# Attention and a multiplicative feed-forward on one core: q of batch 1 turned by transfers, the x product on other PSUM tiles, another listing, the last block of out cut at column 320

## The chip, the core and the metric

The kernel runs on one core of one Trainium2 chip. The metric is the device time of one execution in microseconds (us).

## The reference

```python
q_s = softmax over d of q          # (8 batches, 8 heads, 576 tokens, 64)
k_s = softmax over the tokens of k
kv  = einsum('bhsd,bhse->bhde', k_s, v)
x   = einsum('bhsd,bhde->bhse', q_s, kv)  ->  (4608 tokens, 512)
out = ((x @ w1) * (x @ w2)) @ w3 @ w_out  # w1, w2: 512x1024, w3: 1024x1024, w_out: 1024x512
```

Both softmaxes subtract a maximum and add 1e-9 to the sum. Inputs and the output are float32.

## The kernel before

Every step of the kernel has a name, and the order in which all steps are emitted is written out by hand in the listing `ORDER` (lines 77 to 146). Each engine runs its own steps in the order of that listing; where a step can run on one of several engines, the table `PICKS` (lines 154 to 210) names the engine. `Plan.run` walks the listing and emits each step. Nothing is reordered later, so a step that waits holds up everything behind it on its engine.

The steps, by name (the numbers behind a name are batch or chunk, then part):

- **Loads.** `w1`, `w2` (four column pieces each), `w3` (six row pieces), `wo` (two halves of w_out), `k.b`, `q.b`, `v.b`. The first batches and all weights are issued by POOL in the order of the table `LOADS` (line 217); a load waits until the one eight places before it has landed (line 433). The two parts of q of batch 0 and, later, the batches of the table `LATE` (line 224) are issued by SP. The first of LATE, `q.2`, waits for the load `w1.3`. A batch in the table `APART` (line 265) is loaded in two halves.
- **The fold.** For each of the eight row blocks `ft` of w3: `w3t` transposes it on PE, `w3T` copies that to SBUF, `pf.ft.0` and `pf.ft.1` (four matmuls of 512 columns each) multiply it with the two halves of w_out, and `W3O` moves the result to SBUF. After that out = ab @ W3O, with ab = (x @ w1) * (x @ w2).
- **Attention of batch b.** For k: `kmx` (maximum over a partition's nine tokens; for b below 4 a tree of four DVE instructions, L498 to L501), `cba`, `cbx`, `cb` (maximum across partitions), two `ksub`, two `kexp`. For v: `vc` casts. `kv` multiplies (L549), `kve` and `kv2` divide by the sum. For q, in two parts p (part 0 has four of nine token groups, part 1 has five): `qmx`, `qsub`, `qexp`, `qsm`, `qeps`, `qrc`, `qn`. The normalised q (tile `en`) is then transposed: either `qt` on PE into PSUM (L634) and `qT` back to SBUF, or `qd`, one DMA transpose issued by SP (L642). The table `DMAT` (line 319) says which.
- **The x product.** `xm.b.0` and `xm.b.1` (two PSUM tiles each) and `xt.b` for the last 64 tokens; `xs` and `xts` move them to SBUF. `XRING` (line 654) names the PSUM tiles that they take: `att` (2 banks), `po` (2 banks) or `pab` (4 banks).
- **Chunk c (512 tokens; chunk 8 is all the last tokens together).** `up.1.c.sub.u` = x @ w2 and `up.0.c.sub.u` = x @ w1 for one or two blocks of 128 features, each into one of four `pab` banks (L784, 8 matmuls of 256 columns in chunks 0 and 1, which have two halves `sub`; 4 matmuls of 512 columns in the others). `bs` moves the first to SBUF (L325), `ab` multiplies the second with it (L799, DVE). `down.c.tb` multiplies 128 tokens of ab with W3O (L806, for the last chunk L821, 8 matmuls of 512 columns), `os` moves that to SBUF and `st` stores it.

A `pab` bank comes free when the `bs` or `ab` that reads it is done. The `up` of column piece u of chunks 0 and 1 needs the load of the same piece of w1 or w2.

DVE and POOL steps that use a port which the two share are chained: for the first 580 steps of the listing, such a step on one engine waits for the last such step on the other that stands ahead of it (`link`, line 891). `kmx` trees, `qsub`, `ksub`, `qn`, POOL's `vc` and DVE's `qeps` are such steps.

Of the kernel before, what the change touches and what calls it, by code (L numbers as in the profile page):

```python
# [77 lines left out]
q.0.1 qmx.0.1 qsub.0.1 qexp.0.1 q.0.0 ident w3.4 w3t.5 qmx.0.0 qsm.0.1 wo.0 wo.1 w3.2 k.0 w3.0 w3.3  # L78
w3.5 w3t.4 w3T.5 w3.1 w3T.4 qeps.0.1 qsub.0.0 qrc.0.1 qexp.0.0 qn.0.1 v.0 pf.5.0 pf.4.0 pf.5.1 w3t.2
qsm.0.0 k.1 w2.0 w3T.2 W3O.5 q.1.0 qt.0.16 qt.0.8 qT.0.8 pf.4.1 qT.0.16 qeps.0.0 qrc.0.0 qn.0.0 w1.0  # L80
pf.2.0 pf.2.1 w3t.0 W3O.2 W3O.4 w3T.0 qt.0.0 w3t.3 pf.0.0 w3T.3 w2.1 pf.0.1 pf.3.0 w3t.7 kmx.0.0
cba.0 cbx.0 w1.1 pf.3.1 W3O.0 w3T.7 w3t.1 pf.7.0 w3t.6 w1.2 w2.2 cb.0 ksub.0.1 ksub.0.0 kexp.0.1
kexp.0.0 pf.7.1 qT.0.0 kv.0 W3O.3 w3T.1 W3O.7 kve.0 pf.1.0 pf.1.1 w3T.6 kv2.0 xm.0.0 pf.6.0 pf.6.1
xs.0.0.1 kmx.1.0 xs.0.0.0 xm.0.1 xs.0.1.0 xs.0.1.1 up.1.0.0.0 bs.0.0.0 xt.0 qmx.1.0 k.2 w2.3 cba.1
cbx.1 up.0.0.0.0 up.1.0.1.0 up.0.0.1.0 W3O.1 bs.0.1.0 ab.0.0.0 up.1.0.0.1 up.0.0.0.1 w1.3 v.1
qsub.1.0 qexp.1.0 q.1.1 q.2 xts.0.0 bs.0.0.1 up.1.0.1.1 ab.0.1.0 cb.1 up.0.0.1.1 up.1.0.0.2 qsm.1.0
ksub.1.1 bs.0.1.1 ab.0.0.1 up.0.0.0.2 up.1.0.1.2 qeps.1.0 xts.0.1 qrc.1.0 qn.1.0 bs.0.0.2 ab.0.1.1
ab.0.0.2 kmx.2.0 cba.2 bs.0.1.2 kexp.1.1 up.0.0.1.2 up.1.0.0.3 up.0.0.0.3 up.1.0.1.3 bs.0.0.3 W3O.6
qd.1.0 cbx.2 ab.0.0.3 ksub.1.0 down.0.0 ab.0.1.2 cb.2 vc.1.1 kexp.1.0 vc.1.0 os.0.0 ksub.2.1
up.0.0.1.3 down.0.1 ksub.2.0 qmx.1.1 qsub.1.1 kv.1 bs.0.1.3 os.0.1 kve.1 kexp.2.1 kexp.2.0 ab.0.1.3  # L90
down.0.2 kv2.1 xm.1.0 down.0.3 xs.1.0.1 xs.1.0.0 up.1.1.0.0 up.0.1.0.0 up.1.1.0.1 qmx.2.1 qmx.2.0
os.0.2 qsub.2.1 qexp.1.1 bs.1.0.0 qsm.1.1 qsub.2.0 v.2 up.0.1.0.1 up.1.1.0.2 qexp.2.1 ab.1.0.0
vc.2.1 qeps.1.1 up.0.1.0.2 vc.2.0 qsm.2.1 bs.1.0.1 qexp.2.0 qeps.2.1 kv.2 qrc.1.1 bs.1.0.2 ab.1.0.1
up.1.1.0.3 up.0.1.0.3 kve.2 ab.1.0.2 qn.1.1 qrc.2.1 kv2.2 qsm.2.0 qt.1.8 os.0.3 qt.1.16 bs.1.0.3
ab.1.0.3 down.1.0 qeps.2.0 qn.2.1 qrc.2.0 qT.1.16 qT.1.8 xm.1.1 xs.1.1.0 k.3 down.1.1 st.0.0 st.0.1
q.3 xs.1.1.1 xt.1 xts.1.0 k.4 qd.2.1 qmx.3.0 qmx.3.1 up.1.1.1.0 qn.2.0 bs.1.1.0 xts.1.1 qd.2.0
kmx.3.0 cba.3 up.0.1.1.0 up.1.1.1.1 up.0.1.1.1 ab.1.1.0 xm.2.0 xs.2.0.0 bs.1.1.1 xs.2.0.1 cbx.3
ab.1.1.1 cb.3 up.1.1.1.2 up.0.1.1.2 bs.1.1.2 xm.2.1 xs.2.1.0 xs.2.1.1 up.1.1.1.3 up.0.1.1.3 ab.1.1.2
qsub.3.1 qsub.3.0 qexp.3.0 up.1.2.0.0 up.0.2.0.0 bs.1.1.3 kmx.4.1 ab.1.1.3 qexp.3.1 bs.2.0.0 qsm.3.0
os.1.0 ab.2.0.0 qsm.3.1 qeps.3.0 up.1.2.0.1 up.0.2.0.1 bs.2.0.1 ab.2.0.1 v.3 st.0.2 q.4 up.1.2.0.2  # L100
# [827 lines left out]
```

## Time and profile before

| what | value |
|---|---|
| median of 3 runs | 239.25 us (239.14 to 239.61) |
| the profiled execution's own time | 239.21 us |
| its span in the profile | 237.4 us |
| PE busy | 230.1 us of the span |
| DVE, ACT, POOL busy | 180.3, 121.7, 110.0 us |

The profile shows one execution. A row of the timeline gives start, duration, engine, line, operation, output and input tile and how many instructions were merged; in brackets stands the idle time of the engine before it and what ended it. Matmuls are pipelined, so that the rows of two neighbours overlap; the time that one step costs PE is the distance from its start to the next start. 1.8 us of the execution's own time lie outside the span.

### The profile page before, as it was taken

Reading aid. Unit: us, or ns where it says so; the run is one execution under the profiler, and the core shown is the slowest. Engines: PE = TensorE matmul, PEld = TensorE weight load, DVE = VectorE, ACT = ScalarE, POOL = GpSimd, SP = SyncE. Lnnn points to the kernel's source line nnn. Section 1 sums busy time; section 2 is a strip of 40 time slices with the busy share of each in tenths; the row PEclk is TensorE's granted clock in tenths of the full one; section 3 lists DMA queues with packets and bytes.
Section 4 is the critical chain, followed back from the end, with each engine's and each line's share of the span. In section 5 each row is a group of like instructions: output and inputs, shape, how many; then the busy total and the mean of one; then the engine's idle time right before and its main releaser. Section 6 shows DMA issues by size and latency. Waiting matters only on the chain.

```text
span 237.4 us, 4860 instructions
## 1 busy us (share of the span) xinstructions
PE 230.1 (97%) x1935; PEld 119.5 (50%) x1935; DVE 180.3 (76%) x277; ACT 121.7 (51%) x221; POOL 110.0 (46%) x73
## 2 busy tenths in 40 slices
PE   7889999999999999999999999999999999999994
...
GB/s 207 214 307 209 306 245 300 328 299 382 401 226 309 405 217 179 385 132 282 242 113 281 387 338 95 51 135 0 3 91 52 0 179 2 32 145 88 3 132 133
DMA packets 38742, 46.51 MB, mean 196 GB/s; under 512 B 17088, under 2 KB 22976, under 8 KB 38720
## 3 DMA queue, kind: packets, MB, share of 16 engines
...
q8 instruction: 15, 0.25, 0.4%
...
## 4 chain that ended last, share of the span: by engine, by line
PE 81%; DMA 8%; DVE 5%; POOL 4%; issue 1%; ACT 0%; POOLq 0%; ACTq 0%
PE pab L784 46%; PE po L806 22%; DMA w<-in_moe_w_dram 6%; PE po L457 4%; PE po L821 3%; PE pkv L549 2%; DMA qT<-en 2%; PE xm L667 1%; DVE qm L582 1%; POOL k L524 1%; PE w3t L445 1%; POOL en L619 1%; POOL w L406 1%; DVE ab L799 1%; DVE kmx L498 1%
## 5 line engine op out<-in xcount | busy, mean ns | idle before, releaser
L784 PE MATMUL pab<-x,w1sb 128*128 128x512 f16 (+1 forms) x320 | 65.9, 337 | 0.4 <-DVE kmx L499 0.4
L784 PE MATMUL pab<-x,w2sb 128*128 128x512 f16 (+1 forms) x320 | 66.0, 337 | 0.0
L799 DVE TENSOR_TENSOR ab<-pab,bsb 128x512 f16<-128x512 f32 x72 | 48.6, 682 | 20.2 <-PE pab L784 13.6
L806 PE MATMUL po<-W3O,ab 128*128 128x512 f16 x256 | 58.9, 379 | 0.0
L784 PEld LDWEIGHTS <-w1sb 128*128 128x128 f16 x352 | 34.2, 98 | 28.5 <-DMA w1sb<-in_moe_w_dram 0.6
L784 PEld LDWEIGHTS <-w2sb 128*128 128x128 f16 x352 | 33.5, 98 | 27.5 <-issue 0.7
L325 ACT CAST bsb<-pab 128x512 f16<-128x512 f32 x46 | 26.8, 582 | 35.8 <-PE pab L784 34.6
L524 POOL TENSOR_TENSOR k<-k,cb 128x1152 f32<-128x1152 f32 x12 | 31.4, 2628 | 16.4 <-issue 5.1
L806 PEld LDWEIGHTS <-ab 128*128 128x128 f16 x256 | 24.5, 98 | 28.5 <-issue 0.4
L587 POOL TENSOR_TENSOR q<-q,qm 128x1024 f32<-128x1024 f32 (+1 forms) x14 | 29.5, 2125 | 13.1 <-DVE rc L573 5.4
L325 ACT COPY osb<-po 128x512 f32<-128x512 f32 (+1 forms) x25 | 14.3, 571 | 40.3 <-PE po L806 26.8
L619 POOL TENSOR_TENSOR en<-eq,qr 128x1024 f16<-128x1024 f16 (+1 forms) x13 | 27.2, 2106 | 10.5 <-DVE qr L612 10.4
L582 DVE TENSOR_REDUCE qm<-q 128x20 f32<-128x1280 f32 (+1 forms) x16 | 21.2, 1340 | 3.6 <-DMA q<-in_q_dram 3.6
L325 DVE CAST bsb<-pab 128x512 f16<-128x512 f32 x26 | 17.6, 677 | 6.8 <-PE pab L784 6.3
L600 DVE TENSOR_REDUCE qr<-eq 128x20 f32<-128x1280 f16 (+1 forms) x16 | 21.5, 1341 | 1.5 <-ACT eq L595 1.4
L595 ACT ACTIVATE eq<-q 128x1280 f16<-128x1280 f32 (+1 forms) x16 | 18.5, 1161 | 4.8 <-DVE q L587 3.9
L532 ACT ACTIVATE ek<-k 128x1152 f16<-128x1152 f32 x16 | 18.2, 1163 | 3.8 <-POOL k L524 3.8
L489 DVE TENSOR_REDUCE km<-k 128x128 f32<-128x1152 f32 x8 | 16.9, 2149 | 0.0
L457 PE MATMUL po<-wosb,w3T 128*128 128x512 f16 x64 | 15.3, 379 | 0.5 <-DMA wosb<-in_moe_w_out_dram 0.5
L325 DVE COPY osb<-po 128x512 f32<-128x512 f32 x12 | 8.3, 688 | 9.1 <-PE po L806 7.9
L329 ACT ACTIVATE x<-xm 128x512 f16<-128x512 f32 x18 | 10.3, 597 | 6.4 <-PE xm L667 6.2
L325 ACT CAST v<-v 128x1152 f16<-128x1152 f32 x9 | 10.3, 1148 | 0.3 <-DMA v<-in_v_dram 0.3
...
## 6 DMA issues: line engine op xcount, KB each, us to landing
out_dram<-osb SPq DMA_DIRECT2D x66, 128.0 KB, 2.6
q<-in_q_dram SPq DMA_DIRECT2D x5, 1152.0 KB, 7.7
v<-in_v_dram SPq DMA_DIRECT2D x5, 1152.0 KB, 8.9
k<-in_k_dram SPq DMA_DIRECT2D x4, 1152.0 KB, 10.1
k<-in_k_dram POOLq DMA_DIRECT2D x3, 1152.0 KB, 14.1
v<-in_v_dram POOLq DMA_DIRECT2D x1, 1152.0 KB, 13.9
...
```

The costliest lines, as they stand in the source:

```text
L325: return [(nc.scalar.copy if eng == "ACT" else engine[eng].tensor_copy)(out=out, in_=in_)]
L457: nc.tensor.matmul(st["pf", ft], lhsT=st["w3T", ft][:, gt, :], rhs=wosb[:, gt, :], start=(gt == 0), stop=(gt == N_FT - 1))
L524: return [engine[eng].tensor_tensor(out=kb[:, two(hp), :, :], in0=kb[:, two(hp), :, :], in1=st["cb", b][:, two(hp), None, :].broadcast_to( ...
L532: nc.scalar.activation(out=st["ek", b][:, hp, :, :].rearrange("p j (i d) -> p i j d", i=2), in_=kb[:, two(hp), :, :], func=AF.Exp)
L582: dve.tensor_reduce(out=st["qm", b][:, :, j], in_=qb[:, :, j, :], axis=AX.X, op=ALU.max)
L587: return [engine[eng].tensor_tensor(out=qb[:, :, j, :], in0=qb[:, :, j, :], in1=st["qm", b][:, :, j, None].broadcast_to([P, HH, n, D]), op ...
L595: nc.scalar.activation(out=st["eq", b, p], in_=qb[:, :, j, :], func=AF.Exp)
L600: dve.tensor_reduce(out=st["qr", b][:, :, slice(*PARTS[p])], in_=st["eq", b, p], axis=AX.X, op=ALU.add)
L619: return [engine[eng].tensor_tensor(out=st["en", b][:, j, :, :].rearrange("p j h d -> p h j d"), in0=st["eq", b, p], in1=st["qr", b][:, :, ...
L784: nc.tensor.matmul(st["p", one, c, sub, u][:, a * (t1 - t0):(a + 1) * (t1 - t0)], lhsT=w[:, ct, fb * P:(fb + 1) * P], rhs=x()[:, ct, t0:t1 ...
L799: dve.tensor_tensor(out=st["ab", c][:, nf * u:nf * u + nf, t0:t1], in0=cut(st["p", 0, c, sub, u]), in1=cut(st["bsb", c, sub, u]), op=ALU.mult)
L806: nc.tensor.matmul(st["po", c, tb], lhsT=st["ab", c][:, ft, tb * P:(tb + 1) * P], rhs=W3O[:, ft, :], start=(ft == 0), stop=(ft == N_FT - 1))
```

## The change

- `DMATS` 1 to 0 and `DMATP` to an empty list: both parts of q of batch 1 are transposed by `qd`. Before, part 0 was, and part 1 went through PE (`qt.1.8`, `qt.1.16`) and the copies `qT.1.8` and `qT.1.16`.
- `XRING`: for batches 3 to 7, `xm.b.0` takes `pab` banks in place of `att` banks. Together with `xt.b`, which had them already, half of the tiles of `xm` and all of `xt` of these batches lie on `pab`.
- q of batch 7 is loaded in one piece.
- The last block of out is computed and stored in 320 and 192 columns in place of 256 and 256.
- The listing, the table of engines and the orders of the loads are others throughout. The core of it is shown; the rest differs in the same way.

```diff
 LOADS
-    ("w3", 4), ("wo", 0), ("wo", 1), ("w3", 2), ("k", 0), ("w3", 0), ("w3", 3), ("w3", 5),
-    ("w3", 1), ("v", 0), ("k", 1), ("w2", 0), ("q", 1, 0), ("w1", 0), ("w2", 1), ("w1", 1),
-    ("w1", 2), ("w2", 2), ("k", 2), ("w2", 3), ("w1", 3), ("v", 1), ("q", 1, 1),
+    ("w3", 4), ("w3", 0), ("wo", 0), ("wo", 1), ("k", 0), ("w3", 3), ("w3", 2), ("w3", 5), ("v",
+    0), ("w3", 1), ("k", 1), ("q", 1, 0), ("w2", 0), ("w1", 0), ("w2", 1), ("w1", 1), ("k", 2),
+    ("w2", 2), ("w1", 2), ("w2", 3), ("w1", 3), ("v", 1), ("q", 1, 1),
 LATE
-    ("q", 2), ("v", 2), ("k", 3), ("q", 3), ("k", 4), ("v", 3), ("q", 4), ("v", 4), ("q", 5),
+    ("q", 2), ("k", 3), ("v", 2), ("q", 3), ("v", 3), ("k", 4), ("v", 4), ("q", 4), ("k", 5),
...
-    APART = [("q", 7), ("k", 7), ("v", 7)]
+    APART = [("k", 7), ("v", 7)]
-    DMATS = 1
+    DMATS = 0
-    DMATP = [(1, 0)]
+    DMATP = []
-            return "pab" if name[0] == "xt" else "po" if name[2] else "att"
+            return "po" if name[0] == "xm" and name[2] else "pab"
-                cuts = [0, C // 2, C] if tb == 3 else [0, C]
+                cuts = [0, 320, C] if tb == 3 else [0, C]
```

The listing where chunk 0 and 1 run, before:

```text
kexp.0.0 pf.7.1 qT.0.0 kv.0 W3O.3 w3T.1 W3O.7 kve.0 pf.1.0 pf.1.1 w3T.6 kv2.0 xm.0.0 pf.6.0 pf.6.1
xs.0.0.1 kmx.1.0 xs.0.0.0 xm.0.1 xs.0.1.0 xs.0.1.1 up.1.0.0.0 bs.0.0.0 xt.0 qmx.1.0 k.2 w2.3 cba.1
cbx.1 up.0.0.0.0 up.1.0.1.0 up.0.0.1.0 W3O.1 bs.0.1.0 ab.0.0.0 up.1.0.0.1 up.0.0.0.1 w1.3 v.1
qsub.1.0 qexp.1.0 q.1.1 q.2 xts.0.0 bs.0.0.1 up.1.0.1.1 ab.0.1.0 cb.1 up.0.0.1.1 up.1.0.0.2 qsm.1.0
ksub.1.1 bs.0.1.1 ab.0.0.1 up.0.0.0.2 up.1.0.1.2 qeps.1.0 xts.0.1 qrc.1.0 qn.1.0 bs.0.0.2 ab.0.1.1
ab.0.0.2 kmx.2.0 cba.2 bs.0.1.2 kexp.1.1 up.0.0.1.2 up.1.0.0.3 up.0.0.0.3 up.1.0.1.3 bs.0.0.3 W3O.6
...
```

and after:

```text
pf.7.1 qT.0.0 w2.2 kv.0 w3t.1 w3T.6 kve.0 w1.2 kv2.0 pf.6.0 xm.0.0 w3T.1 W3O.7 kmx.1.0 xs.0.0.0
pf.6.1 pf.1.0 xs.0.0.1 qmx.1.0 xm.0.1 xs.0.1.0 xs.0.1.1 w2.3 w1.3 cba.1 cbx.1 cb.1 up.1.0.0.0 xt.0
up.0.0.0.0 up.1.0.1.0 bs.0.0.0 ab.0.0.0 bs.0.1.0 up.0.0.1.0 up.1.0.0.1 up.0.0.0.1 up.1.0.1.1
qsub.1.0 qexp.1.0 qsm.1.0 W3O.6 v.1 qeps.1.0 ab.0.1.0 qrc.1.0 ksub.1.1 kexp.1.1 q.1.1 kmx.2.0
bs.0.0.1 bs.0.1.1 pf.1.1 up.0.0.1.1 W3O.1 up.1.0.0.2 ab.0.1.1 xts.0.1 ab.0.0.1 up.0.0.0.2 up.1.0.1.2
q.2 bs.0.0.2 ab.0.0.2 cba.2 cbx.2 ksub.1.0 kexp.1.0 bs.0.1.2 xts.0.0 up.0.0.1.2 up.1.0.0.3 qn.1.0
cb.2 bs.0.0.3 ab.0.1.2 up.0.0.0.3 up.1.0.1.3 ab.0.0.3 down.0.0 up.0.0.1.3 vc.1.0 bs.0.1.3 os.0.0
qmx.1.1 vc.1.1 kv.1 kve.1 ksub.2.1 ksub.2.0 ab.0.1.3 kv2.1 qd.1.0 qmx.2.1 qsub.1.1 down.0.1 down.0.2
...
up.1.1.0.0 up.0.1.0.0 up.1.1.0.1 up.0.1.0.1 qeps.1.1 qexp.2.1 os.0.3 qsub.2.0 qrc.1.1 bs.1.0.0
qn.1.1 ab.1.0.0 up.1.1.0.2 up.0.1.0.2 qexp.2.0 bs.1.0.1 qsm.2.1 qeps.2.1 qrc.2.1 up.1.1.0.3 k.3 v.2
q.3 st.0.0 vc.2.0 qd.1.1 st.0.1 st.0.3 ab.1.0.1 qn.2.1 vc.2.1 bs.1.0.2 up.0.1.0.3 kv.2 qsm.2.0
qd.2.1 ab.1.0.2 qeps.2.0 bs.1.0.3 qrc.2.0 ab.1.0.3 down.1.0 qn.2.0 kve.2 kv2.2 xm.1.1 xs.1.1.1
```

146 lines of the change are left out of this document (72 added, 74 removed), and 104 rows, old and new, of the table PICKS.

## The prediction

> **What bounds the kernel now.** I read the page first, then PE by stages, then PE's waits, then the transfers. The page: busy time of the engines, and PE's share of each of 40 slices.
>
> ```profile
> span 237.4 us, 4860 instructions
> PE 230.1 (97%) x1935; PEld 119.5 (50%) x1935; DVE 180.3 (76%) x277; ACT 121.7 (51%) x221; POOL 110.0 (46%) x73
> PE   7889999999999999999999999999999999999994
> ```
>
> PE is the bound. Only its idle time, and work taken off it, can move the end. The stretches (each: length, then busy time of PE, PEld, DVE, ACT, POOL, granted clock, DMA share) say where that idle time is:
>
> ```profile
> 33.49:56.70 23.21, 22.84 (x253) 16.30 (x250) 22.38 (x38) 15.55 (x31) 16.43 (x10) 1.00 1.20 309
> 56.70:73.37 16.67, 16.21 (x211) 12.16 (x210) 15.41 (x25) 11.12 (x20) 13.12 (x7) 1.00 1.00 309
> 73.37:130.00 56.63, 56.63 (x532) 27.57 (x533) 53.77 (x78) 43.83 (x83) 43.08 (x21) 1.00 0.88 256
> 130.00:234.40 104.40, 104.35 (x654) 48.25 (x651) 63.99 (x101) 33.56 (x63) 22.88 (x11) 1.00 0.38 104
> ```
>
> After 73.37 PE is idle for 0.05 us in 161 us, at full clock. So the later listing can only lose, apart from the tail, and gains must come before 73.4. There PE's rows show the steps that matter:
>
> ```profile
> 33.49 1.05 PE L784 MATMUL pab<-x,w2sb 128*128 128x256 f16 x8
> 34.47 0.26 PE L667 MATMUL xt<-qT,kv 64*64 64x64 f16 x8
> 34.66 1.05 PE L784 MATMUL pab<-x,w1sb 128*128 128x256 f16 x8
> ...
> 42.53 1.04 PE L784 MATMUL pab<-x,w2sb 128*128 128x256 f16 x8
> 43.40 1.04 PE L784 MATMUL pab<-x,w1sb 128*128 128x256 f16 x8
> 44.38 1.05 PE L784 MATMUL pab<-x,w2sb 128*128 128x256 f16 x8
> 45.79 1.05 PE L784 MATMUL pab<-x,w1sb 128*128 128x256 f16 x8 [0.36 <-DVE kmx L499]
> ...
> 64.50 0.72 PE L634 MATMUL qtp<-ident,en 128*128 128x128 f16 x10
> 65.06 1.89 PE L806 MATMUL po<-W3O,ab 128*128 128x512 f16 x8
> ...
> 71.87 1.04 PE L784 MATMUL pab<-x,w1sb 128*128 128x256 f16 x8
> 73.37 0.41 PE L667 MATMUL xm<-qT,kv 64*64 64x512 f16 x4 [0.46 <-DMA qT<-en]
> ```
>
> An `up` costs 0.87 us (42.53 to 43.40). Three distances are longer: 43.40 to 44.38 (0.11 lost, `up.1.0.0.3`), 44.38 to 45.79 (0.54 lost, `up.0.0.0.3`) and 71.87 to 73.37 (1.50, less 0.87 and 0.10 for the switch to the small matmuls as at 33.49 to 34.47: 0.53 lost, `xm.2.0`, waiting for its DMA transpose).
>
> The name kmx at 45.79 misleads: `q.2`, which waits for the load `w1.3`, is issued in the same moment, and `up.0.0.0.3` needs `w1.3` too. The transfers (issue rows of POOL and SP; written GB/s in 40 slices of 34.7 to 45.8):
>
> ```profile
> 34.76 0.75 POOL L406 DMA_DIRECT2D v<-in_v_dram  x1 [0.51 <-DMA w1sb<-in_moe_w_dram]
> 45.81 0.37 SPq L406 DMA_DIRECT2D q<-in_q_dram  x1
> 46.23 3.58 SPq L642 DMA_TRANSPOSE qT<-en  x1
> GB/s 199 196 197 192 196 201 199 190 198 192 199 199 225 386 378 389 408 386 482 399 415 448 347 319 221 194 231 188 183 197 199 201 275 362 386 354 415 411 404 448
> ```
>
> `v.1` is issued when `w1.0` has landed: 34.7. A weight piece (0.262 MB written) at some 196 GB/s takes 1.34 us, a k (1.18 MB) at 390 takes 3.0; six pieces and `k.2` make 11.0, and 34.7 + 11.0 is the 45.8 at which `w1.3` is there. Until then the load queue sets when chunk 0 can go on.
>
> **The change, part by part.** *The fold and the load order.* The first 14 loads are the same set in both orders, so `w1.0` lands at 34.7 again, and so do the first 21: `w1.3` at 45.8. Before, the whole fold was done by `up.0.0.0.0` at 34.66, which PE reached with nothing left to do. In the new listing `pf.1.1` stands behind six further `up`; it loses the cover of that wait, and its price is that of four such matmuls:
>
> ```profile
> 24.24 0.86 PE po L457 x4
> ```
>
> +0.86. In between `k.2` now comes two places earlier: `w2.2` lands at 41.7, `w1.2` at 43.1 (before 40.1 and 38.7). PE from 34.66: six `up` (39.9), `pf.1.1` (40.8), `up.0.0.1.1` (41.6). `up.1.0.0.2` waits for `w2.2` and for `bs.0.0.1`, which on ACT stands behind `kexp.1.1`, and that behind `ksub.1.1`:
>
> ```profile
> 39.29 2.61 POOL k L524
> 43.80 1.23 DVE L498 TENSOR_TENSOR kmx<-k 128x1024 f32<-128x1024 f32 x1
> 46.25 0.42 DVE L501 TENSOR_TENSOR km<-kmx,k 128x256 f32<-128x256 f32 x1
> 46.76 2.63 POOL L524 TENSOR_TENSOR k<-k,cb 128x1152 f32<-128x1152 f32 x1 [2.98 <-DVE km L501]
> L532 ACT ACTIVATE ek<-k 128x1152 f16<-128x1152 f32 x16 | 18.2, 1163 | 3.8 <-POOL k L524 3.8
> L799 DVE TENSOR_TENSOR ab<-pab,bsb 128x512 f16<-128x512 f32 x72 | 48.6, 682 | 20.2 <-PE pab L784 13.6
> L325 DVE CAST bsb<-pab 128x512 f16<-128x512 f32 x26 | 17.6, 677 | 6.8 <-PE pab L784 6.3
> ```
>
> `ksub.1.1` began at 39.3, behind `cb.1`. In the new DVE order a W3O, a bs and two ab (0.68 each, less some 0.05 by which neighbours overlap) go behind `cb.1`: up to 2.5 earlier; I take 1.9, as `cb.1` then waits for ACT's `cbx.1`. So `ksub.1.1` starts at 37.4, `kexp.1.1` ends at 41.3 and `bs.0.0.1` at 41.9. PE loses 0.25. `up.0.0.0.2` follows at 42.75 and waits for `w1.2`: 0.35. `up.1.0.1.2` needs the bank that `ab.0.1.1` frees, and that stands behind `kmx.2.0` (43.80 to 46.67: 2.86 us, now from about 40.5, when `k.2`, `ksub.1.1` and `qrc.1.0` are all done): 44.05 against 43.95, 0.1. Then PE runs through to `down.0.0` at 48.4. Its seventh matmul (49.7) needs `ab.0.0.3`, the last of eleven DVE steps behind `kmx.2.0` (five ab, two bs, two xts, cba, cb: 6.5 us from 43.4), 49.9: 0.25. New waits +0.95; the two old ones, 0.11 + 0.54, go: -0.65. At `up.1.1.0.0` PE is 1.1 later than before.
>
> *Transposes of batch 1.* Ten leave PE between 64.50 and 65.06: -0.56. The copies leave DVE and ACT, off the path. SP has one DMA transpose more.
>
> *Landing of these.* The rows: us from issue to landing of `q.2`, of `qd.1.0`, of all thirteen transposes and of `q.3`; and a group of POOL.
>
> ```profile
> q<-in_q_dram SPq DMA_DIRECT2D x1, 1152.0 KB, 7.7
> qT<-en SPq DMA_TRANSPOSE x1, 8.2
> DMA to landing us min/median/max: 3.0/3.7/8.2
> q<-in_q_dram SPq DMA_DIRECT2D x1, 1152.0 KB, 8.3
> L587 POOL TENSOR_TENSOR q<-q,qm 128x1280 f32<-128x1280 f32 x7 | 16.3, 2340 | 9.6 <-DVE qm L582 3.9 <-issue 3.4 <-DVE rc L573 2.2
> ```
>
> `qd.1.0` landed at 54.4, 0.9 behind the `q.2` ahead of it (53.5). `ksub.1.0` on POOL waits for `kmx.2.0` (2.98 us at 46.76 in the rows above) and now starts at 43.4; it and `qn.1.0` (1024 columns, 1.9 by the ratio to the 2.34 of 1280) end at 48.0, where `qd.1.0` is issued: landing 54.4 to 56.2, wanted by `xm.1.0` at 55.7. Bounds 0 and 0.5; I take 0.2. `qd.1.1` is new: POOL from 48.0 has two ksub (5.2), two qsub of 1280 and one of 1024 columns (6.5) and `qn.1.1` (2.3): 62.2. `xm.1.1` wants it at 66.88 + 1.1 - 0.56 = 67.4. Landing after 3.0 to 8.2: 65.2 to 70.4, a wait of 0 to 3.0. `q.3`, ahead on the queue, is issued near 57 (`qsub.1.1` ends at 55.5, its exponential some 1.3 later) and takes 8.3: 65.3, and 0.9 behind it is 66.2; I take 0.2. Behind `xm.1.1` stand `down.1.1`, `xt.1` and all of chunk 1's second half.
>
> [...]
>
> The old wait of `xm.2.0`, 0.53, goes: behind `qn.1.1` POOL has a cast (1.2, as ACT's kexp of the same size), `qn.2.1` and `qn.2.0`, which end at 65.7 and 67.6; the later transpose is in time unless it takes over 5.8 us, and the median is 3.7. -0.53.
>
> *x product on pab.* `xt` lay there already, and PE's idle time is 0.05 in 104 us: I take 0. Bounds 0 and one eviction (0.68, as DVE's CAST) for each of five batches, 3.4.
>
> *Engines exchanged.* DVE gets nine bs more (6 us) after 130, where it has 40 us idle: nothing; without that cover 0.7 each.
>
> *Tail.* Rows: ACT's last copy and the last two stores.
>
> ```profile
> 234.43 0.37 ACT L325 COPY osb<-po 128x256 f32<-128x256 f32 x1 [0.55 <-PE po L821]
> out_dram<-osb SPq DMA_DIRECT2D x2, 128.0 KB, 1.7
> ```
>
> 192 columns in place of 256 take at most a quarter off both, 0.09 and 0.43. The store's 1.7 holds a part that doesn't depend on its size and that no row separates: I take -0.15; bounds 0 and -0.52.
>
> Sum against the execution's own 239.21 (0.04 under the median): +0.86 + 0.95 - 0.65 - 0.56 + 0.2 + 0.2 - 0.53 - 0.15 = +0.32: **239.6** for the median.
>
> **Rivals.** *Transposes late, slower.* Place: SP's queue with `k.3`, `v.2`, `q.3` ahead of `qd.1.1`. It decides once that transpose takes over 5.2 us (67.4 - 62.2). For it: the only one of before with a load 0.4 us ahead took 8.2. Against: `q.3` leaves 5 us earlier. At 7 us PE loses 1.8 in place of 0.2: 241.2. [...]
>
> *The pab banks, slower.* `xm.b.0` holds two of four banks until ACT has moved them; the next `up` waits, 0.3 us a batch for five: 241.1. For it: DVE is busy 53.8 of 56.6 us from 73.4 to 130. Against: PE had no idle time there with `xt` on the same banks.
>
> *The loads are in time, faster.* If `w2.2` and `w1.2` come as early as PE wants them, and ACT and DVE with them, the 0.95 vanish and with them the two 0.2: 238.3. For it: PE's distance at 42.5 in the old trace was clean. Against: the two stretches of 200 and 390 GB/s fit the landing order.
>
> That the change doesn't do what it says is no rival: the ten transposes are gone from PE's instructions and one stands on SP's.
>
> **How the numbers follow.** Forecast (waits exchanged, 239.6, own range 239.2 to 240.2) 0.40; transposes late 0.20; banks 0.15; loads in time 0.25. 0.2% is 0.48 us, about what a measurement here can tell. The forecast lies across that bound: of its 0.40, 0.25 is within and 0.15 slower. Slower 0.15 + 0.20 + 0.15 = 0.50, within 0.25, faster 0.25. Range 238.3 to 241.6: from the third rival to a transpose of 7.5 us.
>
> **What would show it.** PE's distance before the third pair of `up` (0.25, then 0.35), `pf.1.1` at 40; `kmx.2.0` from 40.5; no L634 behind 60; `xm.1.1` and `xm.2.0` without idle time on DMA. A wait of PE on DMA qT over 0.5 us at 67, or rows of pab with idle time after 75, would make it wrong, and so would a head that reaches `up.0.0.0.0` later than 34.7.

## The result and the profile after

| | before | after |
|---|---|---|
| median of 11 runs each | 239.5 us (239.14 to 239.97) | 240.42 us (239.87 to 241.77) |
| ratio to before, 95% interval | | 1.0049 (1.0031 to 1.0066) |
| the profiled execution's own time | 239.21 us | 240.28 us |
| its span | 237.4 us | 238.5 us |

The changed kernel is slower by 0.5%. Two things have to be kept apart in what follows. The profiled execution is 1.07 us longer than the one of before, and this difference can be placed to a tenth. The median moves with what varies between executions, and the changed kernel varies by 1.9 us, the one before by 0.8.

The first lines of the changed kernel's page, its stretches (length, then busy time of PE, PEld, DVE, ACT, POOL, granted clock, DMA share, GB/s) and the rows of PE that answer to those of before. The diff moves the lines of the file by six, so L784 is L790 here, L667 is L673 and L806 is L812; the kernels of the experiments differ by a line or two more.

```profile
span 238.5 us, 4821 instructions
PE 229.7 (96%) x1925; PEld 119.0 (50%) x1925; DVE 179.6 (75%) x277; ACT 118.4 (50%) x216; POOL 116.7 (49%) x76
```

```profile
33.49:56.70 23.21, 23.16 (x257) 16.49 (x250) 21.50 (x38) 14.94 (x28) 19.92 (x11) 1.00 1.20 312
56.70:73.37 16.67, 15.67 (x199) 11.44 (x198) 15.55 (x26) 11.11 (x23) 12.76 (x7) 1.00 1.08 274
73.37:130.00 56.63, 56.63 (x526) 27.67 (x525) 53.29 (x74) 44.21 (x81) 48.16 (x24) 1.00 1.07 318
130.00:234.40 104.40, 104.37 (x658) 47.58 (x656) 65.08 (x105) 29.95 (x61) 19.48 (x10) 1.00 0.33 78
```

```profile
33.65 1.05 PE L790 MATMUL pab<-x,w2sb 128*128 128x256 f16 x8
34.63 0.51 PE L673 MATMUL xt<-qT,kv 64*64 64x64 f16 x8
35.07 1.05 PE L790 MATMUL pab<-x,w1sb 128*128 128x256 f16 x8
...
40.32 1.03 PE L463 MATMUL po<-wosb,w3T 128*128 128x512 f16 x4
41.18 1.04 PE L790 MATMUL pab<-x,w1sb 128*128 128x256 f16 x8
42.06 1.04 PE L790 MATMUL pab<-x,w2sb 128*128 128x256 f16 x8
43.02 1.05 PE L790 MATMUL pab<-x,w1sb 128*128 128x256 f16 x8
44.07 1.03 PE L790 MATMUL pab<-x,w2sb 128*128 128x256 f16 x8
...
48.43 1.89 PE L812 MATMUL po<-W3O,ab 128*128 128x512 f16 x8
50.16 1.04 PE L790 MATMUL pab<-x,w1sb 128*128 128x256 f16 x8
...
55.39 0.41 PE L673 MATMUL xm<-qT,kv 64*64 64x256 f16 x8
...
57.47 1.04 PE L790 MATMUL pab<-x,w2sb 128*128 128x256 f16 x8
...
65.29 1.90 PE L812 MATMUL po<-W3O,ab 128*128 128x512 f16 x8
68.19 0.41 PE L673 MATMUL xm<-qT,kv 64*64 64x256 f16 x8 [1.00 <-DVE qm L588]
...
74.15 0.41 PE L673 MATMUL xm<-qT,kv 64*64 64x512 f16 x4
```

PE stands idle for a microsecond in one place, ahead of `xm.1.1` (68.19). The name in the bracket, a maximum on DVE, has nothing to do with it: `xm.1.1` reads the turned q, kv2 and the att banks, and the transfer `qd.1.1` is what was late (in the profiles of three later runs the bracket at the same step does name the transfer). The issue of `q.3` and of `qd.1.1` by SP, and then their landing, in us from the issue:

```profile
56.79 0.37 SPq L412 DMA_DIRECT2D q<-in_q_dram  x1
61.95 1.72 SPq L648 DMA_TRANSPOSE qT<-en  x1
```

```profile
q<-in_q_dram SPq DMA_DIRECT2D x1, 1152.0 KB, 7.9
qT<-en SPq DMA_TRANSPOSE x1, 6.1
```

`q.3` is there at 64.7, `qd.1.1` at 61.95 + 6.1 = 68.05, and PE wanted it at 67.2.

The other loss lies far behind, in the chain of work that ended last: `xm.5.1`, on the po banks, takes 0.60, where the chain of a run without this wait has 0.22.

```profile
129.80 0.18 PE pab L673 x8
129.99 0.60 PE po L673 x4
```

ACT's copy `os.3.2`, which frees one of the two po banks that `xm.5.1` needs, had waited for an earlier store (the buffers for the results are reused), by the bracket for 0.71 us:

```profile
129.55 0.59 ACT L331 COPY osb<-po 128x512 f32<-128x512 f32 x1 [0.71 <-DMA out_dram<-osb]
```

Laid beside the rows of before, the account of the profiled execution closes: at `up.1.1.0.0` PE is 0.77 later (57.47 against 56.70), at `xm.2.0` 0.78 later (74.15 against 73.37), then 0.42 more is lost to the end of PE's last row (235.54 against 234.34), 0.38 of it at `xm.5.1`, and the tail behind PE is 0.1 shorter: +1.1.

### The profile page after: what moved, and what is told of

Read it like the earlier page. It is cut to its first block, busy times and chain, and to the rows that moved or that the text cites. A ratio compares the mean times of both kernels' runs of the same rounds, so it can differ in the third digit from the quotient of the medians.

```text
span 238.5 us, 4821 instructions
## 1 busy us (share of the span) xinstructions
PE 229.7 (96%) x1925; PEld 119.0 (50%) x1925; DVE 179.6 (75%) x277; ACT 118.4 (50%) x216; POOL 116.7 (49%) x76
## 4 chain that ended last, share of the span: by engine, by line
PE 87%; DMA 6%; DVE 2%; ACT 1%; POOL 1%; issue 0%; POOLq 0%; DVEq 0%; ACTq 0%
PE pab L790 53%; PE po L812 23%; DMA k<-in_k_dram 6%; PE po L463 3%; PE po L827 3%; PE pkv L555 2%; PE xm L673 1%; PE pab L673 1%; PE po L673 1%; POOL w L412 1%; DVE qm L588 1%; DVE kmx L504 1%; PE w3t L451 0%; ACT x L335 0%; POOL wosb L412 0%
## 5 line engine op out<-in xcount | busy, mean ns | idle before, releaser
L790 PE MATMUL pab<-x,w2sb 128*128 128x512 f16 (+1 forms) x320 | 65.9, 337 | 0.0
L790 PE MATMUL pab<-x,w1sb 128*128 128x512 f16 (+1 forms) x320 | 65.9, 337 | 0.0
L805 DVE TENSOR_TENSOR ab<-pab,bsb 128x512 f16<-128x512 f32 x72 | 48.4, 681 | 17.6 <-PE pab L790 8.1
L812 PE MATMUL po<-W3O,ab 128*128 128x512 f16 x256 | 58.6, 379 | 0.0
L790 PEld LDWEIGHTS <-w1sb 128*128 128x128 f16 x352 | 34.1, 98 | 28.5 <-issue 0.6
L790 PEld LDWEIGHTS <-w2sb 128*128 128x128 f16 x352 | 33.8, 98 | 28.2 <-issue 1.3
L593 POOL TENSOR_TENSOR q<-q,qm 128x1024 f32<-128x1024 f32 (+1 forms) x15 | 31.6, 2111 | 17.8 <-DVE qm L588 13.0
L812 PEld LDWEIGHTS <-ab 128*128 128x128 f16 x256 | 24.6, 98 | 29.1 <-issue 0.4
L625 POOL TENSOR_TENSOR en<-eq,qr 128x1024 f16<-128x1024 f16 (+1 forms) x14 | 29.6, 2124 | 18.4 <-DVE qr L618 16.6
L331 ACT CAST bsb<-pab 128x512 f16<-128x512 f32 x37 | 21.2, 582 | 34.5 <-PE pab L790 28.7
L530 POOL TENSOR_TENSOR k<-k,cb 128x1152 f32<-128x1152 f32 x13 | 34.0, 2630 | 5.9 <-DMA k<-in_k_dram 2.6
L331 ACT COPY osb<-po 128x512 f32<-128x512 f32 (+1 forms) x26 | 15.0, 575 | 37.9 <-PE po L812 18.4
L331 DVE CAST bsb<-pab 128x512 f16<-128x512 f32 x35 | 23.8, 680 | 6.8 <-PE pab L790 6.4
L331 DVE COPY osb<-po 128x512 f32<-128x512 f32 (+1 forms) x11 | 7.4, 670 | 14.5 <-PE po L812 9.7
L520 ACT COPY mx<-mx 32x8 f32<-32x8 f32 x32 | 6.3, 196 | 8.0 <-DVE mx L514 7.7
```

Of the source, the lines that this page charges most:

```text
L331: return [(nc.scalar.copy if eng == "ACT" else engine[eng].tensor_copy)(out=out, in_=in_)]
L530: return [engine[eng].tensor_tensor(out=kb[:, two(hp), :, :], in0=kb[:, two(hp), :, :], in1=st["cb", b][:, two(hp), None, :].broadcast_to( ...
L593: return [engine[eng].tensor_tensor(out=qb[:, :, j, :], in0=qb[:, :, j, :], in1=st["qm", b][:, :, j, None].broadcast_to([P, HH, n, D]), op ...
L625: return [engine[eng].tensor_tensor(out=st["en", b][:, j, :, :].rearrange("p j h d -> p h j d"), in0=st["eq", b, p], in1=st["qr", b][:, :, ...
L790: nc.tensor.matmul(st["p", one, c, sub, u][:, a * (t1 - t0):(a + 1) * (t1 - t0)], lhsT=w[:, ct, fb * P:(fb + 1) * P], rhs=x()[:, ct, t0:t1 ...
L805: dve.tensor_tensor(out=st["ab", c][:, nf * u:nf * u + nf, t0:t1], in0=cut(st["p", 0, c, sub, u]), in1=cut(st["bsb", c, sub, u]), op=ALU.mult)
```

## The experiments

In all of them the kernel before ran on the same chip (17 to 29 times for a group, medians 239.41 to 239.49), and the ratio is to it. The changed kernel did not run again, so that others are compared with it through these ratios and the medians of the groups. "The changed kernel" without more is the one above.

### pf.1.1 put back, alone

```diff
-pf.6.1 pf.1.0 xs.0.0.1 qmx.1.0 xm.0.1
+pf.6.1 pf.1.0 pf.1.1 xs.0.0.1 qmx.1.0 xm.0.1
...
-bs.0.0.1 bs.0.1.1 pf.1.1 up.0.0.1.1 W3O.1 up.1.0.0.2
+bs.0.0.1 bs.0.1.1 up.0.0.1.1 W3O.1 up.1.0.0.2
```

> The changed kernel with pf.1.1 put back right behind pf.1.0, ahead of the first up. The prediction's step (pf.1.1 lost the cover of a wait for w1.0, 0.86) expects that PE does it in that wait again: up.1.0.0.2 at 41.2 in place of 42.06, 0.9 us faster, 239.5. The theory after the result: in the changed kernel PE does not wait for w1.0 at all (up.0.0.0.0 at 35.07 waits 0.25 for the copy xs.0.1.1 on ACT only), so the six up shift by the 0.86 that pf.1.1 takes, up.1.0.0.2 stays at 42.0 to 42.1 and the time is the same within 0.2 us, 240.4.

Measured: 240.36 us (239.04 to 242.67, 10 runs), ratio 1.0019 (1.0001 to 1.0036). PE's rows from `up.0.0.1.1` on:

```profile
40.49 1.04 PE L788 MATMUL pab<-x,w1sb 128*128 128x256 f16 x8
41.78 1.03 PE L788 MATMUL pab<-x,w2sb 128*128 128x256 f16 x8 [0.25 <-ACT bsb L329]
43.39 1.05 PE L788 MATMUL pab<-x,w1sb 128*128 128x256 f16 x8 [0.58 <-DMA w1sb<-in_moe_w_dram]
...
48.64 1.89 PE L810 MATMUL po<-W3O,ab 128*128 128x512 f16 x8
...
67.33 0.41 PE L671 MATMUL xm<-qT,kv 64*64 64x256 f16 x8
```

`up.0.0.1.1` comes 0.69 earlier (40.49 against 41.18), so that `pf.1.1` did find cover in the head of this execution, for most of its 0.86. But `up.1.0.0.2`, which waits for `bs.0.0.1`, is only 0.28 earlier, not 0.9, and even this is given back at once: `up.0.0.0.2` waits for the load `w1.2`, and `down.0.0` starts at 48.64, later than the 48.43 of the changed kernel. So the place of `pf.1.1` is not what costs. What neither theory had is the last row: no idle time ahead of `xm.1.1`. In this execution `qd.1.1`, issued at the same time (61.93), landed 4.5 us later in place of 6.1, and its own time is 239.12, as short as the kernel before. So the 1.0 us is in some profiles and not in others. The times of this run fall into two groups (four of 239.04 to 239.63, five of 240.31 to 240.79, and one of 242.67), as such a wait would have it. That the groups are this wait is not shown, since a run has a profile of one execution only, and two of the longer five had a mean granted clock of 0.993, as a stretch at half the clock gives (the last section); and none of the eleven times of the changed kernel itself is below 239.87.

### The head: w3.0 behind wo, alone and with pf.1.1

```diff
 LOADS
-    ("w3", 4), ("w3", 0), ("wo", 0), ("wo", 1), ("k", 0),
+    ("w3", 4), ("wo", 0), ("wo", 1), ("w3", 0), ("k", 0),
 ORDER (fold steps of row blocks 0 and 4 exchanged)
-w3t.5 ... w3t.0 ... w3t.4 ... pf.5.0 ... pf.0.0 ... pf.5.1 ... pf.0.1 ... pf.4.0
+w3t.5 ... w3t.4 ... pf.5.0 ... pf.4.0 pf.5.1 w3t.0 ... pf.4.1 ... pf.0.0 ... pf.0.1
```

> The changed kernel with the load w3.0 put behind the two halves of wo, and the fold steps of row blocks 0 and 4 exchanged so that PE starts with the two blocks of w3.4 as before. Theory: the 1.05 us of PE work missing ahead of 33.49 come from w3.0, loaded second, which shares the transfers with w3.4 and holds back wo; so the first w3t starts at 8.9 (9.47 in the changed kernel), the first pf at 11.4 to 11.6 (13.28), and PE reaches up.1.0.0.0 about 1 us earlier, at 32.6 to 32.9. There the landing of w1.0 (34.7) then stops it: up.0.0.0.0 at 34.7 (35.07), so the time falls by 0.4 us, to 240.0, with pf.1.1 still without cover. Rival: the copies on ACT and DVE set the pace of the fold, not the loads; then up.1.0.0.0 stays at 33.5 to 33.7 and the time at 240.4.

> Both: the head as in the run before and pf.1.1 right behind pf.1.0. Theory: pf.1.1 now does fill the wait for w1.0, so up.1.0.0.2 comes 0.9 to 1.2 us earlier than the 42.06 of the changed kernel, at 40.9 to 41.2, and what the later loads w2.2 and w1.2 (landing 41.7 and 43.1 by the prediction) take back shows as distances over 0.87 us there: 0.5 to 1.2 us faster than the changed kernel, 239.2 to 239.9. Rival (no wait for w1.0 exists, whatever the head): both changes simply add to nothing more than the head alone, up.1.0.0.2 no earlier than in the run before.

Measured: 240.29 us (239.12 to 240.95, 12 runs), ratio 1.0027 (1.0010 to 1.0043), and with `pf.1.1` 239.94 us (238.9 to 240.86, 11 runs), ratio 1.0015 (0.9998 to 1.0031). In the head alone, PE reached `up.0.0.0.0` at 34.85 and then

```profile
43.43 1.05 PE L788 MATMUL pab<-x,w1sb 128*128 128x256 f16 x8 [0.55 <-DMA w1sb<-in_moe_w_dram]
```

`down.0.0` started at 48.68, in the run with both at 48.40. The theory of the head falls in both its parts: the first `pf` did start 1.4 us earlier (11.86 against 13.28), but later pieces stopped PE again (0.45 us for wo at 14.20, 0.20 and 0.45 for w3 at 15.42 and 19.56), `up.1.0.0.0` came at 33.44, 0.21 earlier, and what was left was taken by the wait for `w1.2`, or, in the run with both, by 0.53 us of waiting for `bs.0.0.1` one step ahead. Each head and each place of `pf.1.1` comes to `up.0.0.0.2` at nearly the same time: 43.02 (the changed kernel), 43.39, 43.43, 42.98.

At `xm.1.1` the two differ like the changed kernel and the run before. In the head alone PE does not wait there (67.37, `qd.1.1` landed 4.5 us after its issue); in the run with both it does, with a landing of 6.1:

```profile
68.15 0.41 PE L671 MATMUL xm<-qT,kv 64*64 64x256 f16 x8 [0.96 <-DVE qm L586]
```

### q.3 behind qd.1.1

```diff
-q.3 st.0.0 vc.2.0 qd.1.1 st.0.1 st.0.3
+vc.2.0 qd.1.1 q.3 st.0.0 st.0.1 st.0.3
```

> The changed kernel with the load q.3 and the store st.0.0 issued by SP behind the transpose qd.1.1 in place of ahead of it. Theory: the 1.0 us of idle time ahead of xm.1.1 come from the load, 1.2 MB in the same queue, that lands only at 64.7; without it qd.1.1 lands 3.5 to 4.5 us after its issue at 62, and xm.1.1 starts at 67.0 to 67.3 without a wait (68.19 in the changed kernel). Price: q.3 lands at 71 to 72, DVE wants it at 66.7 (qmx.3.1), stands until then, and PE loses 2 to 5 us behind 72 for want of freed banks: 242 to 245. Rival: ten blocks take 6 us from issue to landing on their own; then the idle time ahead of xm.1.1 stays at 1.0 and the loss behind it comes on top.

Measured: 244.13 us (243.75 to 244.88, 4 runs), ratio 1.0204 (1.0185 to 1.0223). PE's row at `up.0.0.0.0`, at `xm.1.1`, and the stretch in which time was lost:

```profile
34.72 1.05 PE L788 MATMUL pab<-x,w1sb 128*128 128x256 f16 x8 [0.23 <-DMA w1sb<-in_moe_w_dram]
...
67.44 0.41 PE L671 MATMUL xm<-qT,kv 64*64 64x256 f16 x8
...
76.43 0.64 PE L671 MATMUL xm<-qT,kv 64*64 64x512 f16 x4 [2.96 <-DMA qT<-en]
77.00 1.89 PE L788 MATMUL pab<-x,w2sb 128*128 128x256 f16 x8
```

`xm.1.1` had no wait, as the theory said, though one profile alone would not prove it after the run with `pf.1.1`. The price came elsewhere than expected: not on DVE, but at `xm.2.0`, whose transposes now stood behind `q.3` and the stores in SP's queue; SP issued them 2.3 us later (68.65 against 66.35), and the last of them landed 5.6 us after its issue (3.5 in the changed kernel). So most of the 3.0 us is the order in which SP issues, one step on. The last row is a second cost: the matmuls behind the wait ran at half the clock (the last section), and this, too, is in the 244.13. The first row is a find by the way: with a head that came early enough, `up.0.0.0.0` did wait for `w1.0`, at 34.7, as the prediction had it.

### q.3 on ACT's queue, and the stores behind

```diff
-                st[name] = (nc.sync if queue == "SP" else g_).dma_start(
+                st[name] = (nc.scalar if name == ("q", 3) else nc.sync if queue == "SP" else g_).dma_start(
 ORDER
-qexp.1.1 xs.1.0.1 ... k.3 v.2 q.3 st.0.0 vc.2.0 qd.1.1
+k.3 v.2 qexp.1.1 xs.1.0.1 q.3 ... st.0.0 vc.2.0 qd.1.1
```

> The changed kernel with the load q.3 issued by ACT, behind its copy xs.1.0.1, in place of by SP; nothing else moves on SP's queue. Theory: qd.1.1 lands 6.1 us after its issue in some executions and 4.5 in others because its queue has the 1.2 MB of q.3 ahead of it; with q.3 on another queue it lands 4.5 us or less after its issue at 61.9, xm.1.1 starts at 67.2 to 67.5 without idle time in the profile, and the median falls by 0.7 to 1.0 us, to 239.4 to 239.7 (ACT's 0.5 us for the issue cost PE nothing). Rival: the 16 DMA engines are shared whatever the queue, or it is the stores behind it that delay it; then idle time of 1.0 stays in about half of the executions, median 240.3 to 240.5.

And, as the other reading of the late landing, with `q.3` left where it was:

```diff
-qd.1.1 st.0.1 st.0.3 ... qd.2.1 ... qd.2.0
+qd.1.1 ... qd.2.1 ... qd.2.0 st.0.1 st.0.3
```

> The changed kernel with the stores st.0.1 and st.0.3, which SP issues right behind qd.1.1, put behind qd.2.0. Theory of this run: the data of qd.1.1 pass in two bursts with a pause of 1 us between, and the 0.5 MB of the stores issued meanwhile get ahead of the second burst; without them the landing is 4.5 us or less after the issue in every execution, xm.1.1 without idle time, median 239.4 to 239.7. Theory of the run before (the load ahead decides): idle time of 1.0 stays in about half of the executions, median 240.3 to 240.5.

Measured: with `q.3` on ACT 239.74 us (239.13 to 240.94, 12 runs), ratio 1.0017 (0.9999 to 1.0036). With the stores moved 241.07 us (239.8 to 244.19, 12 runs), ratio 1.0067 (1.0046 to 1.0088). The profile of the first is of one of its longest executions (240.94), with a head that was a microsecond late (half the clock from 12 to 15, see the last section):

```profile
68.41 0.41 PE L671 MATMUL xm<-qT,kv 64*64 64x256 f16 x8 [0.43 <-DMA qT<-en]
```

The issue of `q.3` took 0.41 us on ACT. `qd.1.1` was issued at 62.73 there and landed 5.5 us later. So the median moved by the 0.7 of the theory, though the interval still touches that of the changed kernel (0.9999 to 1.0036 against 1.0031 to 1.0066), and the landing was not the 4.5 or less of it: the load's place in the queue may matter, and it isn't all. The stores behind are out as the cause of the late landing: with them moved it was 6.1, as before, and the time rose.

The profile of the run with the stores moved is of its longest execution (244.19). It shows what the stores do elsewhere: `os.3.2` waited 2.37 us for a store there (0.71 in the changed kernel), and `xm.5.1` for `os.3.2`:

```profile
132.47 0.40 PE L671 MATMUL po<-qT,kv 64*64 64x512 f16 x2 [1.24 <-ACT osb L329]
```

### k.2 put back

```diff
 LOADS
-    ("w1", 1), ("k", 2), ("w2", 2), ("w1", 2), ("w2", 3), ("w1", 3),
+    ("w1", 1), ("w2", 2), ("w1", 2), ("k", 2), ("w2", 3), ("w1", 3),
 ORDER (with the head and pf.1.1 of the run with both)
-ksub.1.1 kexp.1.1 q.1.1 kmx.2.0 bs.0.0.1 ... bs.0.0.2 ab.0.0.2 cba.2 cbx.2 ksub.1.0 kexp.1.0 bs.0.1.2
+ksub.1.1 bs.0.0.1 kexp.1.1 q.1.1 ksub.1.0 ... bs.0.0.2 ab.0.0.2 bs.0.1.2 kmx.2.0 cba.2 cbx.2 kexp.1.0
 PICKS
-bs_0_1_2 DVE
+bs_0_1_2 ACT
```

> The head of the second run with pf.1.1 behind pf.1.0 (as in the third), and the load k.2 put back behind w1.2; with it, on DVE, kmx.2.0 behind ab.0.0.2, on ACT bs.0.0.1 ahead of kexp.1.1 and bs.0.1.2 ahead of cbx.2, and ksub.1.0 ahead of kmx.2.0. Theory: all five traces have up.0.0.0.2 at 43.0 to 43.5, whatever the head, because the load w1.2 lands there since k.2 goes ahead of it; with k.2 behind, it lands at 41.7 or earlier and PE runs from 35.3 without a wait to up.0.0.0.3 at 45.8 (46.68 in the changed kernel), where w1.3 lands, and down.0.0 at 47.5 (48.43): 0.9 us. xm.1.1 is then wanted at 66.3 and waits for qd.1.1, which is no earlier than 66.4, so that of the 0.9 at most 0.9 and at least nothing reach the end: 239.2 to 240.2. Rival: w1.2 is not what stops PE; then up.0.0.0.2 stays at 43.0 to 43.5 and down.0.0 at 48.4 to 48.7.

Measured: 241.55 us (241.25 to 242.7, 6 runs), ratio 1.0094 (1.0071 to 1.0117). PE's rows, and DVE's first of `kmx.2.0`:

```profile
36.19 1.05 PE L788 MATMUL pab<-x,w1sb 128*128 128x256 f16 x8
...
48.43 1.46 PE L810 MATMUL po<-W3O,ab 128*128 128x512 f16 x6
52.12 0.61 PE L810 MATMUL po<-W3O,ab 128*128 128x512 f16 x2 [2.24 <-DVE ab L803]
```

```profile
44.97 1.21 DVE L502 TENSOR_TENSOR kmx<-k 128x1024 f32<-128x1024 f32 x1
```

The head was 1.1 late in this execution (half the clock from 10 to 13, see the last section), yet `down.0.0` starts at 48.43 like that of the changed kernel: the fourteen `up` between 36.19 and 48.43 take 12.24 us, 0.874 each, without a wait. By itself that proves little, since the late PE wanted `w1.2` only at 43.19, about when it has landed in the other runs, too. The order of the loads and ACT's rows say more: counted from the 34.7 of `w1.0` at 1.34 us for a weight piece, both read off the profile before, `w1.2` is there at 40.1, an estimate, since no row of this run shows its landing; and the copy `bs.0.0.1` started 4.6 us behind `up.0.0.0.0`, in place of 6.3. With `k.2` behind `w1.2` and `bs.0.0.1` ahead of `kexp.1.1`, the two causes of the waits in chunk 0 are gone. But the place that the edit gives to `kmx.2.0`, 4.4 us later than in the changed kernel (where it started at 40.54), puts `ab.0.0.3` behind it, and `down.0.0` stands 2.24 us for that. So a gain of 0.9 in chunk 0 is likely, though the late head hides it here, and more than that was given back a little later. The early `k.2` is thus an exchange: it costs PE 0.55 to 0.94 at `up.0.0.0.2` in the three profiles whose bracket there names `w1.2`, and keeps the maximum of batch 2 out of the way of `down.0.0`.

### The cut of the last block, alone

```diff
-                cuts = [0, C // 2, C] if tb == 3 else [0, C]
+                cuts = [0, 320, C] if tb == 3 else [0, C]
```

(in the kernel before)

> The kernel before with the last block of out cut at 320 and nothing else. Theory (the prediction's term, -0.15, and the 0.10 read off the two profiles): from the end of PE's last row to the end of the span 2.9 us in place of 3.0, the time 0.05 to 0.15 us shorter, which three digits of a median can hardly show. Rival: a store's time does not depend on its size and nothing is gained (0.0), or the larger first piece is late and costs 0.2.

Measured: 239.39 us (238.88 to 240.04, 12 runs), ratio 0.9997 (0.9984 to 1.0011). In its profile PE's last row ends at 226.99 + 7.09 = 234.08 and the span at 237.0: 2.9 us. The same sum gives 3.1 for the kernel before (227.25 + 7.09, span 237.4) and 3.0 for the changed one (228.45 + 7.09, span 238.5). About 0.1, as small as expected, and no median shows it.

### The transposes of batch 1 alone

In the kernel before:

```diff
-    DMATS = 1
+    DMATS = 0
-    DMATP = [(1, 0)]
+    DMATP = []
 ORDER
-qn.1.1 ... qt.1.8 ... qt.1.16 ... down.1.0 ... qT.1.16 qT.1.8 xm.1.1 ... k.3 ... st.0.0 st.0.1 q.3 ... k.4
+qn.1.1 ... k.3 st.0.0 st.0.1 q.3 k.4 qd.1.1 down.1.0 ... xm.1.1
```

> The kernel before with the first edit alone: part 1 of q of batch 1 is turned by a DMA transpose, issued by SP as soon as qn.1.1 is done, behind the loads k.3, q.3, k.4 and two stores; the ten transposes and their copies leave PE, DVE and ACT. Theory: PE wants xm.1.1 0.56 earlier, at 66.3 (66.88 before); qn.1.1 ends at 64.1 there (61.9 in the changed kernel, where the listing moves it), so that the landing, 4.5 to 6.1 us after the issue, comes at 68.6 to 70.2 and PE waits 2.3 to 3.9 us: 0.56 saved, 241.2 to 242.8 in the end, less what the wait of xm.2.0 (0.5) absorbs. So the edit is only worth anything with the new listing's earlier qn.1.1. Rival: with POOL late, the transpose lands in the median 3.7 us and the loss is below 1.0, 239.8 to 240.3.

Measured: 244.28 us (243.85 to 245.45, 4 runs), ratio 1.0209 (1.0180 to 1.0238). PE's rows and two stretches (granted clock in the third place from the end):

```profile
70.55 0.41 PE L665 MATMUL xm<-qT,kv 64*64 64x256 f16 x8 [3.12 <-DMA qT<-en]
70.90 3.33 PE L804 MATMUL po<-W3O,ab 128*128 128x512 f16 x8
```

```profile
71.50:72.50 1.00, 1.00 (x4) 0.42 (x3) 0.93 (x3) 0.59 (x2) 0.20 (x1) 0.50 1.17 181
75.50:78.00 2.50, 2.50 (x25) 2.15 (x22) 0.69 (x1) 1.35 (x3) 1.01 (x1) 1.00 1.00 371
```

The wait, 3.12, is inside the 2.3 to 3.9 of the theory; the time is above it, because the wait brought a second cost: PE came back at half the clock, and `down.1.1` took 3.33 us in place of 1.90. The first edit without the new listing is a loss of 2%; with it, and with `qn.1.1` ended at 61.9, the whole change is within a microsecond of break-even.

### Sums of edits

First the head, `pf.1.1`, `q.3` on ACT and, new, `xm.5.1` off the po banks:

```diff
         def XRING(name):
             if name[1] < XMS:
                 return "att"
+            if name == ("xm", 5, 1):
+                return "att"
             return "po" if name[0] == "xm" and name[2] else "pab"
```

> The changed kernel with three of the edits together: the head of the third run (w3.0 behind wo, pf.1.1 behind pf.1.0), q.3 issued by ACT, and xm.5.1 on the att banks in place of the po banks. Theory: the third run gave 239.94 and the one with q.3 on ACT's queue 239.74, against 240.42; the gains lie at different places (chunk 0, xm.1.1) and add in part, as an earlier chunk 0 reaches xm.1.1 earlier and the landing of qd.1.1 does not move: 239.3 to 239.6. The idle time ahead of the up behind xm.5.1 (0.4 in the changed kernel's profile, 0 to 0.25 in three others) is 0 in the profile, since xm.5.1 no longer needs both po banks and so not os.3.2, which waits for a store. Rival: xm.5.1 waits for its transpose, then the 0.2 to 0.4 can appear on att too. For a kernel that beats both it would have to come out at 239.2 or less.

Then two more, and a third on top of them:

```diff
 LATE
-    ("q", 2), ("k", 3), ("v", 2), ("q", 3),
+    ("q", 2), ("v", 2), ("k", 3), ("q", 3),
 ORDER
-ksub.1.1 kexp.1.1 q.1.1 kmx.2.0 bs.0.0.1
+ksub.1.1 q.1.1 kmx.2.0 bs.0.0.1 kexp.1.1
 ORDER (third edit)
-qd.1.1 st.0.1 st.0.3 ... qd.2.1 ... qd.2.0
+qd.1.1 ... qd.2.1 st.0.1 ... qd.2.0 st.0.3
```

> The kernel of the run with three edits together, with two more: SP issues the load v.2 ahead of k.3, and on ACT bs.0.0.1 stands ahead of kexp.1.1. In that run's profile POOL waited 0.81 us for v.2 (vc.2.0), which put the transposes of batch 2 back and gave PE 0.65 us of idle time ahead of xm.2.0; and up.1.0.0.2 waited 0.24 for bs.0.0.1. Theory: v.2 lands 2 us earlier, POOL does not wait, xm.2.0 starts without idle time; chunk 0 gains 0.2 to 0.4, so far as w1.2 has landed; xm.1.1 is reached at 66.4 to 66.6 and still finds its transpose landed (61.6 + 4.5 = 66.1). 0.5 to 0.9 faster than the 239.35 of that run: 238.5 to 238.9, ahead of the kernel before. Rival: what is taken out ahead comes back as a wait for qd.1.1 or for w1.2; then 239.2 to 239.5, no better than before.

> The run beside it, with the store st.0.1 put behind qd.2.1 and st.0.3 behind qd.2.0 on SP, so that no store stands ahead of a transpose of batch 2 that is ready. Theory: qd.2.1 and qd.2.0 are issued as soon as qn.2.1 and qn.2.0 end; 0 to 0.3 us, since POOL and not SP sets these, 238.4 to 238.9. Rival: the run that moved both stores had 1.2 us of idle time at xm.5.1 (on po banks there, on att here) and 241.07; if late stores hold up a copy os elsewhere, PE waits again and the time is 239.5 or more.

Measured: 239.35 us (238.69 to 240.97, 12 runs), ratio 1.0005 (0.9988 to 1.0022); 239.41 us (238.98 to 240.16, 12 runs), ratio 1.0000 (0.9987 to 1.0014); and 240.18 us (239.48 to 240.81, 12 runs), ratio 1.0029 (1.0015 to 1.0044). `xm.1.1` and `xm.5.1` in the first, `up.0.0.0.2` and `xm.2.0` in the second:

```profile
66.83 0.41 PE L673 MATMUL xm<-qT,kv 64*64 64x256 f16 x8
...
129.18 0.39 PE L673 MATMUL xm<-qT,kv 64*64 64x512 f16 x4
129.50 1.04 PE L790 MATMUL pab<-x,w1sb 128*128 128x512 f16 x4
```

```profile
43.69 1.05 PE L790 MATMUL pab<-x,w1sb 128*128 128x256 f16 x8 [0.94 <-DMA w1sb<-in_moe_w_dram]
...
73.59 0.41 PE L673 MATMUL xm<-qT,kv 64*64 64x512 f16 x4
```

The first sum gets back the whole loss of the change, and its interval does not meet the changed kernel's: idle time ahead of `xm.1.1` and behind `xm.5.1` is 0 in its profile. How much each of the three edits gives is not separated. The second removes the wait of `xm.2.0` (0.65 in the first) as expected, and the rival comes true as well: what chunk 0 gains ahead is stopped at `w1.2`. The third shows again that a store moved back costs more than it gives: in its profile PE waits 0.68 us at `xm.2.0` again, and 0.54 for a copy `bs` at 131.25. No version here beats the kernel before by more than can be measured.

## Why the prediction was right, and where it wasn't

The forecast was 239.6 us with slower as the likeliest sign, and up to 241.6; measured 240.42. The sign came true and the time is inside the whole range, but above the 239.2 to 240.2 that the forecast gave for itself. The profiled execution's sum was to be +0.32 and is +1.07. The difference is made of terms of both signs: up to `up.1.1.0.0` PE lost 0.77 in place of 1.16, the 0.2 at `qd.1.0` did not come, `qd.1.1` cost 1.0 to 1.1 in place of 0.2, and 0.42 behind `xm.2.0` were not forecast. That the number is not further off is in part luck. By its steps:

- **pf.1.1 without cover, +0.86, and new waits, +0.95.** The time at `down.0.0` is right, its parts aren't: it was forecast at 48.4 and started at 48.43. That PE waited for `w1.0` in the kernel before does not show in its rows: from `xt.0` to `up.0.0.0.0` it took 0.19 (34.47 to 34.66), as at the next `xt` (69.05 to 69.24). Cover there was in the head all the same, where PE waits for pieces of w3 and wo, longer in the changed kernel's profile (1.63, 0.54, 0.36 and 0.42) than before (0.79, 0.50, 0.23 and 0.21): put back there, `pf.1.1` made `up.0.0.0.0` 0.17 later (35.24 against 35.07). But `up.0.0.0.0` was 0.4 late (the prediction named a head later than 34.7 as what would make it wrong): the fold ended 0.16 later (33.65 against 33.49), and `xt.0` takes 0.44 to the next row in place of 0.19, since the copy `xs.0.1.1` is on ACT now in place of DVE (ACT's copies end at 34.83, and the last matmuls of `xt.0` start at 34.9). Against that, of 0.70 us of waits up to 45 only 0.27 appeared (distances of 0.96 and 1.05 at 42.06 and 43.02). Earlier and later cancel because PE meets the same two things a little behind 42, however it gets there: the copy `bs.0.0.1` behind `kexp.1.1`, and the landing of `w1.2`, forecast at 43.1 and seen at 43.4 to 43.7 in the three profiles that name it (by 42.7 in another). Moving `pf.1.1` back showed it: 0.69 gained up to `up.0.0.1.1`, and nothing left at `down.0.0`. The step was sized as a loss of its own, and is a share of these waits.
- **down.0.0 waits for ab.0.0.3, 0.25.** It didn't: 48.43 to 50.16 is 1.73.
- **The old waits of 0.65 gone.** Right; behind 44.07 no distance up to `down.0.0` is longer than 0.88.
- **Ten transposes leave PE, -0.56.** Right: nothing but `kv.2` stands between the last `up` and `down.1.0` at 65.29.
- **qd.1.0, +0.2.** Landed in time (48.0 + 6.3 = 54.3, wanted at 55.4): 0, the lower bound.
- **qd.1.1, +0.2, with bounds 0 to 3.0.** This is the mis-sized term: 1.0 in the profiled execution, 0.96 in the run with both edits of the head and 0.99 in the one with the stores moved, and 0 with `pf.1.1` alone and with the head alone, all with the same queue ahead of it. The forecast took the landing as 0.9 behind `q.3`, from the row of `qd.1.0`. `q.3` landed at 64.7, earlier than the 65.3 assumed, but `qd.1.1` came 3.4 behind it there and 1.9 in the run with `pf.1.1` alone. At 6.1 us the rival "transposes late" has decided (its point was 5.2), as the prediction's 0.20 allowed; at 4.5 it hasn't.
- **xm.2.0, -0.53.** Right here: 74.15 without idle time, 0.78 later than before while it was 1.3 later at `xm.1.1`. It is no fixed gain: with `q.3` on ACT and in two of the sums a wait of 0.55, 0.65 and 0.68 stands there again.
- **x product on pab, 0.** Right for pab: of the 0.42 lost behind `xm.2.0` 0.38 lie at `xm.5.1` on po, which leaves 0.04 for all else. (The 0.03 us of idle time in the last two stretches would not show this alone: the wait at `xm.5.1` lies within a merged row and counts as busy.) What the prediction did not look at is the half that stays on po: `xm.5.1` takes both po banks, and so stands behind `os.3.2`, the last copy of `down.3` that is listed ahead of it, which here waited for a store. From its start to the next `up` PE takes 0.32 where nothing waits (129.18 to 129.50 above); it took 0.39 more here, 0.25, 0.25 and 0.30 more in three profiles with the same rings (the head alone, `q.3` on ACT, `k.2` put back), and nothing more in three (`pf.1.1` alone, both edits of the head, `q.3` behind `qd.1.1`). With the stores moved the wait for `os.3.2` was 1.24, and on att there was none. So the store as the cause is supported by one execution in which it came later still; an edit that moves nothing but this store was not tried, nor was the exchange of rings alone.
- **Tail, -0.15.** 0.1, and not to be seen in a median. Little of a store's time goes with its size here: the last two, 160 and 96 KB, landed 1.8 and 1.6 us after their issue, those of 128 KB before after 1.7.

Of the two theories on the late transpose, the stores behind are refuted and the load ahead in SP's queue is supported, not shown. With `q.3` ahead of it in SP's queue `qd.1.1` landed after 3.5, 4.5, 4.5, 5.6, 6.1, 6.1 and 6.1 us in seven profiles; with `q.3` on ACT after 4.3, 4.6, 4.6 and 5.5 in four. The lower times with `q.3` elsewhere agree with the load ahead as the cause, the 5.5 is not explained by it, and of the 3.0 us at `xm.2.0` with `q.3` and the stores put ahead 2.3 are SP's later issue. No profile showed this transpose land in under 3.5 us.

One thing goes with the late landing in all eleven of these profiles: SP's own row for the issue takes 1.38 to 1.51 us in the six with 4.6 or less, and 1.65 to 2.38 in the five with 5.5 or more. That would put what makes it late ahead of the stores behind it, which are issued later. Why one execution has 4.5 and another 6.1, with issues at the same time to 0.1 us, stays open.
